# One unit's sums moved to TensorE, a norm's sum folded into a square, and a new order: a gated linear recurrence with a feed-forward block on one core

## The chip, the cores and the metric

The kernel runs on one core of a Trainium2 chip. A core has five engines with queues of their own: TensorE (PE in the profile, with its weight loads as PEld), VectorE (DVE), ScalarE (ACT), GpSimd (POOL) and SyncE (SP), which here only issues DMAs. The metric is device time in microseconds of one execution; before the change three runs took 679.76, 679.85 and 688.25 us, median 679.85.

## What is computed

An attention-like recurrence feeds a feed-forward block. For each of 4 x 8 heads of dimension 48, with S = 768 steps:

```
scale = min(|a|, 0.999) / (|a| + 1e-6)          # a = a_re + i a_im, per step and channel
S_t   = (a_t * scale_t) S_{t-1} + k_t v_t^T      # complex state, 48 x 48
y_t   = q_t . Re(S_t)
x     = y as 3072 rows of 384 (8 heads x 48)
out   = relu(x @ w_in)^2 @ w_out                 # w_in 384 x 2048, w_out 2048 x 384
```

The two weight matrices arrive as 64-bit floats and are turned to 32 bits on the core.

## The kernel before

The 3,072 rows are worked in six **units** (n = 0 to 5) of 512 rows. In a unit a partition holds W = 4 neighbouring steps of all heads; the heads are in two **halves** z of four, and in four **pairs** of heads. A unit goes through these stages, named by their functions.

`load` brings a_re, a_im (tile aq, first part), q and k (aq, second part) in from SyncE's queue (L910), for unit 0 with a_im from ScalarE's queue; v comes from GpSimd's queue (L925). `roots` takes the square of the modulus (L948, or L963 and L968 in unit 0; L971), then the logarithm (L973), an exponential with -0.5 (L975) for a first 1/|a|, its square (L977), and two VectorE steps (L979, L983) that refine it. In unit 0 the first half is cut in two, so that L973 to L983 run three times there. `normalise` makes the scale from it (L989 to L1003). At L1006 ScalarE squares the refined 1/|a| once more into a tile nobody reads, `junk`, only for the sum that such an activation can leave in the table `sums`. Such sums are tested at the end by `verdict`: if one is out of bounds, a slower general path runs instead.

`inner` multiplies the decays within a partition in two rounds: `terms` (L1021) makes the four partial products of a complex product, `joined` (L1025, L1026) takes their difference and sum. The second round's result goes to the tile xn. `totals` turns xn on TensorE with a permuted identity, `perm` (`turned`, L1070), and ScalarE copies the result to e (L1084, L1087). `scan` then runs a prefix product over e on VectorE (from L1159), `back` turns the result back, `factors` and `inverse` make reciprocals, and `apply` forms the scaled q and k (L1299 to L1327). `pairs` gathers keys (KC, L1370), transposes (by TensorE in unit 0, L1434; by VectorE and DMA to QT afterwards, L1410 and L1415), takes scores (L1456), masks them (L1462), keeps the state (L1486 to L1498) and mixes the output (L1510, L1514); ScalarE copies it out (L1520) and SyncE stores it to xT (L1528), the feed-forward block's input. `squares` sums q, k and v squared for the same test (L1268, L1271).

`dense` is the feed-forward block, twice per unit on 256 rows: w_in's products (L1570), relu and square on ScalarE (L1602, L1603), and w_out's products, plainly in unit 0 (L1617), by a scheme with seven half products and sums on VectorE afterwards (L1679, L1694, L1703). The weights are fetched in 8 + 8 pieces on GpSimd's queue (L820) and converted on ScalarE (L833, L837) and VectorE (L839, L843, L846). At the end `inspect` fetches them again and tests their range.

**What sets the order.** No stage is issued as it is written. Each call of `step`, `check` or `dma` adds a step to a plan: its engine, an assumed duration, what it reads and writes, and a rank. When the program is built, `Plan.order` plays the steps through with these assumed durations; whenever an engine is free it takes, of the steps that are ready, the one of lowest rank. The result fixes the order in each engine's queue, DMA issues included; the queues are in order on the chip. Ranks come from the stage and the unit (CHAIN 2, PAIR 1, DENSE 3, times 100), and `plan.shift` (L1821) adds numbers to single steps, counted in the order in which they are added, and to groups of them (same engine, same line, same rank). Where the plan has TensorE wait, it puts in idle matmuls of identity by identity (L738). VectorE runs the planned queue for unit 0 among the conversions of weights.

Of the kernel before, what the change touches and what calls it, by code (L numbers as in the profile page):

```python
# [632 lines left out]
def fast_path(ctx, tc, q, k, v, a_re, a_im, moe_w_in, moe_w_out, out, flag):  # L633
# [6 lines left out]
    C = 128  # L640
# [62 lines left out]
    NS = 11  # L703
# [168 lines left out]

    def parts(n):

        t, got = n * L, []
        while t < (n + 1) * L:
            b, s = divmod(t, S)
            m = min(S - s, (n + 1) * L - t)
            got.append(((t - n * L) // W, m // W, b, s))
            t += m  # L880
        return got
# [46 lines left out]
    def chain(n):  # L928
# [16 lines left out]
        def roots(z):  # L945
# [7 lines left out]
            for u in range(cut):  # L953
# [5 lines left out]
                if n == 0:  # L959
# [17 lines left out]
                step("ACT", ac(size), k(1), k(3), lambda u=u: act.activation(  # L977
                    out=part(t, u), in_=part(f1, u), func=AF.Square), first)
# [8 lines left out]
        def normalise(z):  # L987
# [3 lines left out]
            if n == 0:  # L991
# [14 lines left out]
            check("ACT", ac(Y), key(z, 3), [], lambda: act.activation(  # L1006
                out=junk[:, 0:Y], in_=t, func=AF.Square, saturate=False,
                accum_out=sums[:, n, 2 + z:3 + z]), first)

        def inner(z):  # L1010
# [4 lines left out]
            def pair(x0, x1, o, m, keys):  # L1015
                f1, f2 = (ff[z][:, i * m:(i + 1) * m].rearrange(
                    "p (r h d) -> p r h d", r=2, d=D) for i in range(2))

                def terms():
                    for j, f in enumerate((f1, f2)):  # L1020
                        dve.tensor_tensor(out=f, in0=x0, in1=x1[:, j].unsqueeze(  # L1021
                            1).to_broadcast(list(x0.shape)), op=ALU.mult)

                def joined():
                    dve.tensor_tensor(out=o[:, 0], in0=f1[:, 0], in1=f2[:, 1], op=ALU.subtract)  # L1025
                    dve.tensor_tensor(out=o[:, 1], in0=f1[:, 1], in1=f2[:, 0], op=ALU.add)  # L1026
                step("DVE", 2 * tt(m), [("a", z)], key(z, 0, 1), terms, ahead)
                step("DVE", 2 * tt(m // 2), key(z, 0, 1), keys, joined, ahead)
# [24 lines left out]
        E = [("e", 0), ("e", 1), ("e", 2)]  # L1053
        for fn in (roots, normalise, inner):
            for z in range(2):
                fn(z)
# [22 lines left out]

        def totals(j):  # L1080
            ps, b = turned(lambda m: xn[:, j, ts(m, C)], spread, perm,
                           [("xn", j, 0), ("xn", j, 1)], ahead)
# [183 lines left out]
        def squares(j):  # L1266
            for r in range(2):
                check("ACT", ac(Y), [(("qk", "k")[r], j)], [], lambda r=r: act.activation(  # L1268
                    out=junk, in_=QK[j][:, ts(r, Y)], func=AF.Square, saturate=False,
                    accum_out=sums[:, n, 4 + 2 * j + r:5 + 2 * j + r]), late[j])  # L1270
            check("ACT", ac(Y), [("v", vs(n))], [], lambda: act.activation(  # L1271
                out=junk, in_=vv[vs(n)][:, ts(j, Y)], func=AF.Square, saturate=False,
                accum_out=sums[:, n, 8 + j:9 + j]), late[1])
# [58 lines left out]
        def rest(*zs):  # L1332
# [4 lines left out]
            for z in zs:  # L1337
                twist(z)
                squares(z)
# [421 lines left out]
    def verdict():  # L1761
        def collect():
            for lo, hi, top_ in ((0, 2, 60), (2, 4, 12), (4, NS - 1, 20), (NS - 1, NS, 114)):
# [53 lines left out]
    for i in range(2 * NPIECE):  # L1817
        inspect(i)
    verdict()

    plan.shift(  # L1821
        groups={14: 395.74, 15: 440.83, 22: -2.57, 69: 298.91, 73: -200.67, 80: 0.99, 82: 4.44, 86:
# [5 lines left out]
        single={10: -100.97, 40: -497.42, 44: 62.89, 45: 37.9, 48: 75.39, 51: 100.84, 53: 52.42, 56:  # L1828
# [69 lines left out]
```

## Time and profile before

| | |
|---|---|
| median of three runs | 679.85 us |
| the profiled execution's own time | 680.22 us |
| its span, first to last instruction | 678.4 us |
| mean granted TensorE clock | 0.996 |
| busy: TensorE / its weight loads / VectorE / ScalarE / GpSimd | 657.3 / 592.6 / 557.7 / 350.9 / 111.4 us |
| idle matmuls of L738, within TensorE's busy time | 62.5 us |
| first dense product (L1570) starts | 93.94 us |
| last dense product (L1679) ends | 672.5 us |

A row of groups reads: line, engine, operation, output <- input, shapes, count | busy time in us, mean ns of one | idle time of the engine just before them, and what ended it. A row of the timeline or of the chain begins with start and length in us; in brackets stands the idle time before it with what ended it.

### The profile page before, as it was taken

To read this page: it belongs to the slowest core of one execution; us is meant where nothing else is said; L and a number is where in the kernel's file an instruction comes from. 1 tells how busy PE (TensorE), PEld (TensorE's weight loads), DVE (VectorE), ACT (ScalarE), POOL (GpSimd) and SP (SyncE) were. 2 spreads that over 40 slices of the span, in tenths; PEclk is the share of its full clock that TensorE was granted. 3 is DMA by queue.
4 is the path that set the end of the run, shared out by engine and by line. 5 is a ranking of instruction groups with operands and counts; after the bars stand their busy time and mean duration, and the time that the engine had idled before them with its cause. 6 is when DMAs were issued, how large, how long until landed. Compare 5 with 4: busy or idle time off the path is not lost.

```text
span 678.4 us, 13507 instructions
## 1 busy us (share of the span) xinstructions
PE 657.3 (97%) x5176; PEld 592.6 (87%) x5176; DVE 557.7 (82%) x1157; ACT 350.9 (52%) x574; POOL 111.4 (16%) x191
## 2 busy tenths in 40 slices
PE   9989999999899999999999999999999999999996
PEld 9989878677668998888998988988999989989996
DVE  5999989999499999698999788997889997347631
ACT  6997589962385514557524738334658132131230
POOL 6300305042000021002122030120030120032100
PEclk9999999999999999999999999999999999999999
DMA  9931659237660036624147562156360164287600
GB/s 278 300 121 44 148 139 253 108 104 181 154 166 15 23 74 157 171 67 129 36 123 167 132 139 48 37 141 161 101 179 20 36 153 104 56 300 262 230 2 28
DMA packets 56130, 86.32 MB, mean 127 GB/s; under 512 B 8916, under 2 KB 36640, under 8 KB 56056
## 3 DMA queue, kind: packets, MB, share of 16 engines
q1 hardware_dynamic: 39160, 37.93, 21.8%
q0 software_dynamic: 11840, 41.30, 21.1%
q10 hardware_dynamic: 5056, 6.13, 3.4%
q8 instruction: 43, 0.70, 0.5%
q14 instruction: 31, 0.25, 0.1%
HBM read 48.76 MB, written 4.72 MB: 79 GB/s over the span
## 4 chain that ended last, share of the span: by engine, by line
PE 56%; DVE 25%; DMA 7%; ACT 6%; issue 2%; SPq 1%; ACTq 1%; DVEq 0%
PE d L1570 24%; PE d L1679 22%; DMA QT<-aq 3%; DVE f L1327 3%; PE sc L1456 3%; DMA aq<-in_a_im_dram 2%; PE yp L1510 2%; DVE aq L1410 2%; PE yp L1514 2%; DVE w L846 2%; PE tr L1486 2%; DVE f L1299 1%; PE d L1617 1%; DVE KC L1179 1%; ACT g L1602 1%
## 5 line engine op out<-in xcount | busy, mean ns | idle before, releaser
L1570 PE MATMUL d<-xT,w 128*128 128x256 f32 x1104 | 246.7, 380 | 2.5 <-ACT g L1602 1.1
L1570 PEld LDWEIGHTS d<-xT,w 128*128 128x128 f32 x1104 | 207.6, 190 | 34.0 <-ACT g L1602 2.6
L1602 ACT ACTIVATE g<-d 128x512 f32<-128x512 f32 x92 | 54.8, 595 | 166.9 <-PE d L1570 109.4
L1679 PE MATMUL d<-w,g 128*128 128x192 f32 x640 | 111.6, 327 | 0.0
L1679 PEld LDWEIGHTS d<-w,g 128*128 128x128 f32 x640 | 104.6, 190 | 1.2 <-issue 0.6
L1679 PE MATMUL d<-T,g 128*128 128x192 f32 x480 | 84.6, 328 | 1.9 <-DVE g L1694 1.9
L1679 PEld LDWEIGHTS d<-T,g 128*128 128x128 f32 x480 | 78.7, 190 | 3.0 <-DVE g L1694 2.2
L1694 DVE TENSOR_TENSOR g<-g 128x512 f32<-128x512 f32 x80 | 53.9, 687 | 31.1 <-PE d L1679 17.4
L738 PE MATMUL d<-ident 128*128 128x128 f32 x526 | 62.5, 283 | 1.6 <-POOL ident masks.py:199 1.6
L738 PEld LDWEIGHTS d<-ident 128*128 128x128 f32 x526 | 61.9, 199 | 1.7 <-POOL ident masks.py:199 1.6
L1603 ACT ACTIVATE g<-g 128x512 f32<-128x512 f32 x96 | 60.6, 631 | 3.1
L1640 POOL DMA_DIRECT2D out_dram<-ot x22 | 12.7, 576 | 265.1 <-DVE ot L1703 221.4
L1520 ACT COPY yt<-yp 112x512 f32<-112x512 f32 x24 | 26.6, 1106 | 48.4 <-PE yp L1514 48.4
L1370 POOL DMA_DIRECT2D KC<-f x56 | 34.8, 627 | 101.2 <-DVE f L1327 40.9
L1410 DVE STREAM_TRANSPOSE aq<-f 128x768 f32<-128x768 f32 x40 | 47.8, 1265 | 0.2
L1327 DVE TENSOR_TENSOR f<-aq 128x768 f32<-128x768 f32 (+1 forms) x56 | 44.3, 838 | 0.6
L1617 PE MATMUL d<-w,g 128*128 128x384 f32 x128 | 44.4, 494 | 0.0
L1456 PE MATMUL sc<-QT 96*64 96x128 f32 (+1 forms) x736 | 39.0, 254 | 4.1 <-DMA QT<-aq 1.9
L1456 PEld LDWEIGHTS sc<-QT 96*64 96x64 f32 x736 | 35.6, 138 | 7.6 <-issue 4.0
L1703 DVE TENSOR_TENSOR ot<-ot,d 128x192 f32<-128x192 f32 x70 | 23.6, 349 | 20.6 <-PE d L1679 20.2
L1617 PEld LDWEIGHTS d<-w,g 128*128 128x128 f32 x128 | 24.1, 193 | 14.4 <-issue 0.5
L1021 DVE TENSOR_TENSOR f<-aq 128x768 f32<-128x768 f32 (+1 forms) x48 | 34.2, 752 | 0.5
(190 smaller groups left out, 915.9 us busy)
## 6 DMA issues: line engine op xcount, KB each, us to landing
QT<-aq SPq DMA_DIRECT2D x152, 64.0 KB, 2.5
f<-in_moe_w_in_dram POOLq DMA_DIRECT2D x8, 768.0 KB, 6.9
f<-in_moe_w_out_dram POOLq DMA_DIRECT2D x8, 768.0 KB, 6.4
QT<-aq ACTq DMA_DIRECT2D x76, 64.0 KB, 3.6
out_dram<-ot POOLq DMA_DIRECT2D x22, 192.0 KB, 3.7
KC<-f POOLq DMA_DIRECT2D x20, 192.0 KB, 3.7
xT<-yt SPq DMA_DIRECT2D x36, 96.0 KB, 2.3
aq<-in_q_dram SPq DMA_DIRECT2D x8, 384.0 KB, 5.3
```

What stands on the lines that cost most here:

```text
L738: plan = Plan(lambda b: pe.matmul(bank[b][:, 0:C], lhsT=ident, rhs=ident, start=True, stop=True), ["d2", "d1", "d0"], lambda ap: tc.nc.val ...
L1021: dve.tensor_tensor(out=f, in0=x0, in1=x1[:, j].unsqueeze(1).to_broadcast(list(x0.shape)), op=ALU.mult)
L1327: lambda j=j, r=r, o=o: dve.tensor_tensor(out=o[:, :, :, r * D:(r + 1) * D], in0=qk[:, j], in1=a[:, r], op=ALU.mult), late[z])
L1370: lambda i=i, queue=queue, lo=lo, hi=hi, a0=a0, a1=a1: queue.dma_start(out=kc[lo:hi, i], in_=nat[a0:a1]),
L1410: lambda nat=nat, dst=dst, j=j: dve.transpose(out=dst[:, j], in_=nat), rank)
L1456: pe.matmul(sa[r:r + C // 2, j, :, lo:32], lhsT=T[:, j, 1, h, ts(late, C // 2)], rhs=T[:, j, 0, h].rearrange("p (c t) -> p c t", c=W)[:, : ...
L1570: pe.matmul(ps, lhsT=w1[:, f // FP, m, ts(f % FP, C)], rhs=xT[:, n % 2, m, ts(grp, G)], start=(m == 0), stop=(m == NM - 1))
L1602: act.activation(out=o, in_=ps, func=AF.Relu)
L1603: act.activation(out=o, in_=o, func=AF.Square)
L1617: pe.matmul(ps, lhsT=gt[:, f % 2, ts(i, C)], rhs=w2[:, f], start=(f == 0), stop=(f == NF - 1))
L1679: pe.matmul(bank[b][:, 0:DH], lhsT=g4[:, r, j], rhs=w(j), start=first and j == 0, stop=last and j == NT - 1)
L1694: step("DVE", tt(4 * C), gk(x0, h) + gk(x1, h), gk(o, h), lambda: dve.tensor_tensor(out=g4[:, o, sl], in0=g4[:, x0, sl], in1=g4[:, x1, sl] ...
```

## The change

Three things.

1. The activation at L1006 is dropped. Its place is taken by the square in `roots` (L977), which now leaves its own sum in `sums`. Unit 0 has three of these squares, so the table gets a column more (NS 12), and `verdict` tests the new columns.
2. In unit 0, `joined` of the second round is dropped. `totals` takes the partial products themselves: a new step `joint` multiplies them, on TensorE, by `perm` and by its negative `nperm`, accumulating, so that the difference and the sum come out already turned. It takes twelve matmuls with 64 columns of weights, in turn to the upper and the lower half of the output's partitions, in place of three transposes. ScalarE makes `nperm` once.
3. The numbers of `plan.shift` are others throughout, and with the dropped and added steps they count differently. Queues of the DMAs are not changed: the loads stay on SyncE.

`squares_of` is added but, with AFTER = 0, never called, and `squares` stays as it was but for the column numbers.

```diff
-    NS = 11
+    NS = 12
+    AFTER = 0
...
-                step("ACT", ac(size), k(1), k(3), lambda u=u: act.activation(
-                    out=part(t, u), in_=part(f1, u), func=AF.Square), first)
+                at = 2 + z if u == 0 else 4
+                check("ACT", ac(size) + 0.09, k(1), k(3), lambda u=u, at=at: act.activation(
+                    out=part(t, u), in_=part(f1, u), func=AF.Square,
+                    accum_out=sums[:, n, at:at + 1]), first)
...
-            check("ACT", ac(Y), key(z, 3), [], lambda: act.activation(
-                out=junk[:, 0:Y], in_=t, func=AF.Square, saturate=False,
-                accum_out=sums[:, n, 2 + z:3 + z]), first)
...
-                step("DVE", 2 * tt(m // 2), key(z, 0, 1), keys, joined, ahead)
+                if n or keys == [("a", z)]:
+                    step("DVE", 2 * tt(m // 2), key(z, 0, 1), keys, joined, ahead)
...
+        nperm = yts[0][:, 0:C]
+        if n == 0:
+            step("ACT", 0.25, [], [("yt", 0)], lambda: act.mul(out=nperm, in_=perm, mul=-1.0),
+                 rank)
...
+        def joint(j):
+            b = trs[slot["tr"] % 2]
+            slot["tr"] += 1
+            ps = bank[b][:, 0:DM]
+            f = [ff[z][:, 0:Y].rearrange("p (i r x) -> p i r x", i=2, r=2) for z in range(2)]
+
+            def go():
+                for c0 in range(0, 2 * NM, 2):
+                    for i in range(2):
+                        for c in (c0, c0 + 1):
+                            r = 64 * (c % 2)
+                            pe.matmul(spread(ps[r:r + 64], c // 2),
+                                      lhsT=f[c // NM][:, i, (i + j) % 2, ts(c % NM, 64)],
+                                      rhs=nperm if (i, j) == (1, 0) else perm,
+                                      start=i == 0, stop=i == 1)
+            step("PE", 1.4, key(0, 0, 1) + key(1, 0, 1) + [("yt", 0)], [(b,)], go, ahead, mode=1)
+            return ps, (b,)
+
         def totals(j):
-            ps, b = turned(lambda m: xn[:, j, ts(m, C)], spread, perm,
-                           [("xn", j, 0), ("xn", j, 1)], ahead)
+            ps, b = joint(j) if n == 0 else turned(
+                lambda m: xn[:, j, ts(m, C)], spread, perm, [("xn", j, 0), ("xn", j, 1)], ahead)
...
     plan.shift(
-        groups={14: 395.74, 15: 440.83, 22: -2.57, 69: 298.91, 73: -200.67, 80: 0.99, 82: 4.44, 86:
...
+        groups={3: -336.32, 8: -339.38, 9: 203.68, 15: 194.34, 28: 5.78, 29: -244.11, 91: -4.1, 97:
+            -8.34, 102: -255.12, 103: 422.4, 111: 356.0, 114: -237.11, 116: 2.36, 160: 100.49,
...
+        single={40: 459.41, 43: 446.7, 44: -245.71, 49: -438.55, 58: -1.11, 81: -227.32, 82:
+            -251.41, 83: 100.96, 100: 0.02, 121: 0.61, 143: -221.32, 161: 109.9, 162: -255.4,
```

More of the change, by code (lines that the diff above doesn't have):

```diff
@@ L869, in inspect, with squares_of @@
         check("DVE", ts2(PW) + tt(PW), keys, keys + [("odd",)], look, rank)
+    def squares_of(n, j):
+        z, s = (3 * n + j) % 2, (3 * n + j) // 2 % 2
+        t = ff[z][:, s * Z:(s + 1) * Z]
+        keys = [("f", z, 2 * s), ("f", z, 2 * s + 1)]
+        rank = (LATE, 2 * NPIECE + 3 * n + j)
+        for p0, m, b, at in parts(n):
+            src = (q, k, v)[j][b, :, at:at + m * W, :].rearrange("h (p c) d -> p h (c d)", c=W)
+            dma(pool, [("gate", 1)], keys, lambda p0=p0, m=m, src=src: pool.dma_start(
+                out=t.rearrange("p (h x) -> p h x", h=H)[p0:p0 + m], in_=src),
+                rank, m * 3072 * 2, dur=0.74, group=n)
+        at = (5, 6, 9)[j]
+        check("ACT", ac(Z) + 0.09, keys, keys, lambda: act.activation(
+            out=t, in_=t, func=AF.Square, accum_out=sums[:, n, at:at + 1]), rank)
     def parts(n):
@@ L1269, in squares @@
                     out=junk, in_=QK[j][:, ts(r, Y)], func=AF.Square, saturate=False,
-                    accum_out=sums[:, n, 4 + 2 * j + r:5 + 2 * j + r]), late[j])
+                    accum_out=sums[:, n, 5 + 2 * j + r:6 + 2 * j + r]), late[j])
             check("ACT", ac(Y), [("v", vs(n))], [], lambda: act.activation(
                 out=junk, in_=vv[vs(n)][:, ts(j, Y)], func=AF.Square, saturate=False,
-                accum_out=sums[:, n, 8 + j:9 + j]), late[1])
+                accum_out=sums[:, n, 9 + j:10 + j]), late[1])
         def apply(z, p, np):
@@ L1338, in rest @@
                 twist(z)
-                squares(z)
+                if n >= AFTER:
+                    squares(z)
             for z in zs:
@@ L1762, in collect @@
         def collect():
-            for lo, hi, top_ in ((0, 2, 60), (2, 4, 12), (4, NS - 1, 20), (NS - 1, NS, 114)):
+            for lo, hi, top_ in ((0, 2, 60), (2, 5, 12), (5, NS - 1, 20), (NS - 1, NS, 114)):
                 dve.tensor_scalar(out=ok[:, :, lo:hi], in0=sums[:, :, lo:hi],
@@ L1818, in fast_path @@
         inspect(i)
+    for n in range(AFTER):
+        for j in range(3):
+            squares_of(n, j)
     verdict()
     plan.shift(
-        groups={14: 395.74, 15: 440.83, 22: -2.57, 69: 298.91, 73: -200.67, 80: 0.99, 82: 4.44, 86:
[5 rows of a table removed]
-        single={10: -100.97, 40: -497.42, 44: 62.89, 45: 37.9, 48: 75.39, 51: 100.84, 53: 52.42, 56:
[13 rows of a table removed]
+        groups={3: -336.32, 8: -339.38, 9: 203.68, 15: 194.34, 28: 5.78, 29: -244.11, 91: -4.1, 97:
[5 rows of a table added]
+        single={40: 459.41, 43: 446.7, 44: -245.71, 49: -438.55, 58: -1.11, 81: -227.32, 82:
[11 rows of a table added]
     with tc.manual_schedule():
```

32 rows, old and new, of tables (groups, single) are left out of this document.

## The prediction

> **What bounds the kernel now.** I read the head of the page first, then the timeline of TensorE, then the busy times in stretches cut where that timeline changes, then TensorE's waits.
>
> ```profile
> span 678.4 us, 13507 instructions
> PE 657.3 (97%) x5176; PEld 592.6 (87%) x5176; DVE 557.7 (82%) x1157; ACT 350.9 (52%) x574; POOL 111.4 (16%) x191
> ...
> L738 PE MATMUL d<-ident 128*128 128x128 f32 x526 | 62.5, 283 | 1.6 <-POOL ident masks.py:199 1.6
> ```
>
> TensorE looks full at 97%, but 62.5 us of that are the matmuls of L738, identity times identity, which only fill time while nothing else can run. The timeline of TensorE shows the last of them and the first dense product (L1570):
>
> ```profile
> 90.24 1.38 PE L738 MATMUL d<-ident 128*128 128x128 f32 x10
> ...
> 93.94 3.02 PE L1570 MATMUL d<-xT,w 128*128 128x256 f32 x12
> ```
>
> So I cut at 93.94, at 200 and at 655. In the table of stretches the columns are length, then busy time and count of TensorE, its weight loads, VectorE, ScalarE and GpSimd, the granted clock, the DMA share and GB/s:
>
> ```profile
> 9.30:93.94 84.64, 81.74 (x929) 78.25 (x927) 82.00 (x198) 65.25 (x92) 21.88 (x36) 1.00 0.63 175
> 93.94:200.00 106.06, 100.49 (x657) 75.66 (x656) 91.07 (x171) 71.93 (x116) 22.26 (x33) 0.98 0.59 155
> 200.00:655.00 455.00, 449.94 (x3448) 413.85 (x3445) 375.03 (x770) 207.57 (x357) 64.01 (x102) 1.00 0.43 115
> 655.00:678.40 23.40, 17.49 (x108) 17.20 (x106) 6.96 (x14) 0.91 (x2) 0.00 (x0) 0.96 0.07 22
> ```
>
> There are two stages with different limits. Up to 93.94 it is VectorE: 82.00 of 84.64 us busy, while TensorE fills. From there TensorE is the bound, with real work: it idles 106.06 - 100.49 = 5.57 us up to 200 and 455.00 - 449.94 = 5.06 us up to 655, together 10.63. The last stretch is the closing chain of products and stores. The time is thus the start of the first dense product, plus TensorE's own work, plus 10.63 of stalls, plus an end of fixed length. An edit can gain by an earlier start or by fewer stalls. The stalls have names in the waits of TensorE from 94 to 660 (total, times, longest):
>
> ```profile
> PE d L1679 <- DVE g L1694: 1.9, 1, 1.9
> PE sc L1456 <- DMA QT<-aq: 1.9, 2, 1.0
> ...
> PE sc L1456 <- DMA T<-aq: 0.9, 1, 0.9
> PE sc L1456 <- DMA xT<-yt: 0.8, 1, 0.8
> ```
>
> No single one is over 1.9 us. All sums below are made against the profiled execution, 680.22 us (its span of 678.4 and 1.8 around it); the median of the three runs shown is 679.85, 0.37 lower, which I take off at the end. Two per cent of it is 13.6 us, about what a measurement of this kernel can tell from no change.
>
> **The change part by part.** First the squares. In each unit and half the sum at L1006 goes, and the square at L977 gets an accumulation. The timeline of ScalarE in unit 0:
>
> ```profile
> 16.56 0.84 ACT L977 ACTIVATE f<-f 128x768 f32<-128x768 f32 x1
> 17.31 0.83 ACT L1006 ACTIVATE junk<-f 128x768 fp8e5<-128x768 f32 x1
> 18.05 0.19 ACT L1006 ACTIVATION_READ_ACCUMULATOR junk<-f 128x1 f32 x1
> 18.27 0.84 ACT L992 ACTIVATE junk<-f 128x768 fp8e5<-128x768 f32 x1
> ```
>
> From start to start L1006 takes 18.27 - 17.31 = 0.96 us, the reading of its sum 18.27 - 18.05 = 0.22 of that. Removed 0.96, added 0.22 behind L977: 0.74 less on ScalarE for each of twelve, 8.9 us. In unit 0 there are three squares, since its first half is cut in two: 2 x 0.96 - 3 x 0.22 = 1.26 less. ScalarE is 52% busy, so nearly all of this lies beside TensorE's stream and is worth nothing. The reading may hold L979 on VectorE by 0.22 where nothing else is ready for it; in unit 0 that is three times, 0.66 at most, and I take nothing, since the order has conversions to put there. The gain counts where ScalarE stands on the chain of work, and there L1006 is right ahead of SyncE's store of xT, the transfer that TensorE's wait of 0.8 names:
>
> ```profile
> 189.72 0.83 ACT junk L1006 x2
> 190.55 0.14 SPq L1528
> ```
>
> I take that wait as gone, **-0.8**; its bounds are 0 (another transfer holds the store) and -0.8.
>
> Second, the inner sums of unit 0. VectorE loses four instructions, L1025 and L1026 into xn for both halves. Its timeline:
>
> ```profile
> 25.18 0.35 DVE L1025 TENSOR_TENSOR xn<-f 128x192 f32<-128x192 f32 x1
> 25.45 0.35 DVE L1026 TENSOR_TENSOR xn<-f 128x192 f32<-128x192 f32 x1
> 25.72 0.95 DVE L1000 SCALAR_TENSOR_TENSOR f<-f 128x768 f32<-128x768 f32 x1
> ...
> 35.25 2.80 DVE L846 CUSTOM_DVE_ANT_0 w<-w,w 128x1536 uint16<-128x1536 uint16 x3
> 37.97 0.35 DVE L1159 TENSOR_TENSOR KC<-e 128x192 f32<-128x192 f32 x1
> ```
>
> A pair takes 25.72 - 25.18 = 0.54 us from start to start, two take 1.08. VectorE bounds this stage, so the first dense product comes earlier by **-1.1**. In its place TensorE has two steps of twelve matmuls, 64 columns wide and alternating between the halves of the array, for two steps of three transposes:
>
> ```profile
> 35.09 0.82 PE L1070 MATMUL tr<-perm,xn 128*128 128x128 f32 x6
> 35.74 10.66 PE L738 MATMUL d<-ident 128*128 128x128 f32 x94
> ...
> 74.99 0.93 PE L1456 MATMUL sc<-QT 96*64 96x128 f32 x15
> ```
>
> The transposes take 0.82 / 2 = 0.41 a step. Twelve of the new kind cost at least the spacing of L1456, which alternates halves too, 0.93 / 15 = 0.062 each or 0.74 a step, and at most that of a whole matmul, 10.66 / 94 = 0.113 or 1.36. That is 0.33 to 0.95 more a step, 0.7 to 1.9 for both; the row that is alike gives 0.7. On TensorE it takes the place of fillers. For the scan (L1159) it is a delay. VectorE covered the present gap, 35.25 to 37.97, with three conversions; with the sums gone the gap is some 0.7 longer, and a further conversion or L1039 fits in. Without that cover it costs 0.7 to 1.9; I take 0. The negated matrix is one small ScalarE copy, less than the 1.26 saved there.
>
> Whether going from 64 columns to the whole array and back costs something, TensorE's timeline shows elsewhere:
>
> ```profile
> 66.50 1.96 PE L1434 MATMUL d<-ident,f 128*96 128x128 f32 x16 [0.61 <-DVE f L1327]
> 68.38 1.09 PE L1456 MATMUL sc<-QT 96*64 96x128 f32 x16
> ```
>
> L1456 starts before the end of L1434 (66.50 + 1.96 = 68.46), so a switch shows no gap. The Trainium skill, TensorEngine Tiling (Array Packing), section Key Properties, says that changing the tiling mode drains the TensorE; by it each new step would begin and end with a drain. The trace does not show such a drain as lost time, and fillers stand on both sides, so the sum would be the same unless the scan's cover is gone.
>
> Third, the new order. The two tables at the end count steps, and groups of alike steps, as the code adds them. Counting them through: unit 1's sixteen loads on SyncE go ahead of all else that is ready there (group 114, which had a default place); unit 0's loads of v go ahead of the weight fetches on GpSimd (group 3); w2's conversions on VectorE go far back (group 103); the second half of unit 0 is hurried (singles 81 and 82). The timeline of SyncE shows what issuing two of these loads takes, the chain of work how long the last one takes to land, and VectorE's timeline who waits behind it:
>
> ```profile
> 83.97 1.28 SPq L910 DMA_DIRECT2D aq<-in_a_re_dram  x2
> ```
> ```profile
> 85.30 8.32 DMA aq<-in_a_im_dram
> ```
> ```profile
> 95.34 0.96 DVE L971 TENSOR_TENSOR f<-f 128x768 f32<-128x768 f32 x1 [1.66 <-ACT f L948]
> ```
>
> The load issued at 85.30 lands 8.32 later, and VectorE then idles 1.66 before L971. Loads that are issued sooner end that. It reaches TensorE only through the end of unit 1's attention, so I give it the 0.9 that TensorE waits for T<-aq, **-0.9**. What the rest of the order does, the trace of before cannot show. Its gain is bounded by all stalls, 10.63. Its loss is bounded by the loads: one issue takes 1.28 / 2 = 0.64, sixteen 10.2 us, and if all stand ahead of the last store of xT, the first dense product is that much later. I take 0 for it, since the stalls named above are small, many, and on different engines. The v loads delay weights by what six of them take; conversions are only filler before the scan, so this falls under the cover above.
>
> Sum: 680.22 - 0.8 - 1.1 - 0.9 = 677.4; less 0.37, **677.0 us**.
>
> **The rivals.** *The order closes the stalls*: with the start 1.1 earlier and all 10.63 gone, 679.85 - 11.7 = 668; with VectorE's 84.64 - 82.00 = 2.64 idle in the first stage gone too, 665.5; half of it gives 673. For it speaks that the stalls are waits on moved work; against it that they have many causes.
>
> *SyncE's queue blocks*, the slow one. A load at the head of that queue which waits for its half of aq holds the KC gathers, the xT stores and later the QT transposes behind it. SyncE's timeline has the stores of unit 0's last pairs right behind the loads:
>
> ```profile
> 86.34 12.75 SPq L1528 DMA_DIRECT2D xT<-yt  x8
> ```
>
> The eight take 12.75 us, with waits between them. With all sixteen ahead it costs 10.2, so 687; if units 2 to 5 lose as much again as the 5.06 that they stall now, or double that, 692 to 697. It decides from the point where the loads hold the queue by more than the 2.8 that I gain.
>
> *Nothing arrives*: the removed VectorE time is given back in the longer gap before the scan, and the other waits go to the next transfer; 679.9. The change then doesn't do what it says for the time.
>
> *Weight loads bound TensorE*, not matmuls. PEld is busy 592.6 us, 87%. If the dense stream ran at the load's pace, a better order would shrink it. The chain has a row on its spacing, the groups one on its weight loads:
>
> ```profile
> 633.25 18.13 PE d L1570 x84
> ```
> ```profile
> L1570 PEld LDWEIGHTS d<-xT,w 128*128 128x128 f32 x1104 | 207.6, 190 | 34.0 <-ACT g L1602 2.6
> ```
>
> 18.13 / 84 = 0.216 us a matmul, back to back. A weight load takes 0.190; at that pace 1,104 matmuls of L1570 take 29 us less, 648. Against it: 0.216 stands wherever nothing is waited for, whatever the order. The Trainium Kernel Development and Optimization page of the Trainium skill, section Performance Expectations, holds LDWEIGHTS busy % for the measure, not matmul busy; this trace does not agree for this stream.
>
> **How the numbers follow.** Forecast, 674 to 682: 0.48. Stalls closed, 665 to 673: 0.20. SyncE blocks, 683 to 697: 0.22. Nothing arrives: 0.08. Weight loads: 0.02. Faster by over 2% means under 666.2: the last case and a fifth of the second, 0.06. Slower by over 2% means over 693.4: not quite half of the third, 0.10. The range leaves out the second case below 668 and the fourth rival, 0.07 together, and of the third what lies above 689, 0.13: 668 to 689.
>
> **What would show it.** ScalarE's busy time is lower by 8 to 9 us and L1006 is gone; the four L1025 and L1026 into xn of unit 0 are gone; the new matmuls take 0.7 to 1.4 us a step, and L1159 starts the scan without an idle VectorE ahead of it; the first L1570 starts at 92 to 93.5; TensorE's idle time from there to 655 is 8 to 10.6. I am wrong if that start is past 95 with xT stores behind loads on SyncE, or if the idle time is under 5 or over 13.

## The result: slower by 0.6 per cent

The changed kernel takes 685.44 us in the median (20 runs, 679.3 to 689.94), the kernel before beside it 680.84. The ratio is 1.0056, with a 95% interval of 1.0034 to 1.0078: about 3.8 us slower, where 2.8 faster was forecast. The time lies within the forecast's range, on the other side of no change. Ratios, here and below, leave out the executions in a slower state that some runs fall into, and they are not the quotients of the medians shown, from which they differ by up to 0.3 per cent. The profiled execution took 685.22 us, with a span of 683.5 and a mean granted clock of 0.992. The head of its page, and the groups' row of the idle matmuls (L738 before):

```profile
span 683.5 us, 13541 instructions
PE 657.1 (96%) x5194; PEld 594.6 (87%) x5194; DVE 557.3 (82%) x1153; ACT 342.3 (50%) x564; POOL 110.5 (16%) x191
...
L739 PE MATMUL d<-ident 128*128 128x128 f32 x502 | 59.4, 282 | 1.6 <-POOL ident masks.py:199 1.6
```

ScalarE lost 350.9 - 342.3 = 8.6 us of work, and TensorE, busy for as long as before, does 3 us less of it in idle matmuls. The first dense product (L1609, L1570 before) starts at 98.92, not 93.94. The table of stretches, cut there, at 200, and 23.40 ahead of the end as before:

```profile
9.30:98.92 89.62, 83.37 (x942) 79.79 (x940) 83.01 (x198) 71.73 (x102) 21.47 (x37) 0.96 0.58 166
98.92:200.00 101.08, 91.05 (x560) 69.33 (x560) 83.47 (x159) 59.12 (x99) 22.67 (x33) 0.99 0.58 153
200.00:660.10 460.10, 457.09 (x3543) 420.17 (x3540) 382.26 (x781) 207.19 (x358) 63.64 (x102) 1.00 0.43 116
660.10:683.50 23.40, 17.96 (x111) 17.67 (x109) 6.98 (x14) 1.35 (x3) 0.00 (x0) 0.97 0.07 21
```

TensorE's idle time is 10.03 + 3.01 = 13.04 us, against 10.63. The 5.1 us of span are thus: the start 4.98 later, 2.41 more of stalls, 2.29 less of TensorE's work behind the start (548.14 against 550.43), the end the same. TensorE's waits in the same part now have one large name, the relu and square of ScalarE (L1641, L1602 before):

```profile
PE d L1609 <- ACT g L1641: 7.7, 3, 3.5
PE yp L1549 <- ACT f L1014: 2.7, 1, 2.7
PE tr L1090 <- DVE xn L1268: 1.2, 2, 0.7
```

Where the late start begins is seen in the first microseconds of ScalarE's timeline, before and after:

```profile
0.86 1.52 ACTq L910 DMA_DIRECT2D aq<-in_a_im_dram  x3
```
```profile
2.27 0.31 ACT L1072 ACTIVATE yt<-perm 128x128 f32<-128x128 f32 x1 [0.17 <-POOL perm L722]
2.27 2.20 ACTq L926 DMA_DIRECT2D aq<-in_a_im_dram  x3
```

ScalarE's queue also issues unit 0's a_im loads. The copy that makes `nperm` stands ahead of them, and it waits for `perm`, which GpSimd writes first. So the loads leave at 2.27, not 0.86. VectorE's first square waits for them, before and after:

```profile
4.50 0.56 DVE L968 TENSOR_TENSOR f<-aq 128x384 f32<-128x384 f32 x1 [3.01 <-DMA aq<-in_a_im_dram]
```
```profile
7.65 0.56 DVE L984 TENSOR_TENSOR f<-aq 128x384 f32<-128x384 f32 x1 [6.16 <-DMA aq<-in_a_im_dram]
```

1.41 us at the issue have become 3.15 at the first square. In after SyncE issues its loads of q and k from 2.35, alongside the late a_im loads; that the loads slow each other down would explain the difference, but it was not tested.

### The profile page after: what moved, and what is told of

Read it like the earlier page. It is cut to its first block, busy times and chain, and to the rows that moved or that the text cites. A ratio compares the mean times of both kernels' runs of the same rounds, so it can differ in the third digit from the quotient of the medians.

```text
span 683.5 us, 13541 instructions
## 1 busy us (share of the span) xinstructions
PE 657.1 (96%) x5194; PEld 594.6 (87%) x5194; DVE 557.3 (82%) x1153; ACT 342.3 (50%) x564; POOL 110.5 (16%) x191
## 4 chain that ended last, share of the span: by engine, by line
PE 61%; DVE 23%; DMA 7%; issue 3%; ACT 3%; SPq 2%; ACTq 1%; DVEq 0%
PE d L1609 24%; PE d L1718 24%; PE sc L1495 4%; PE yp L1549 3%; DMA aq<-in_k_dram 2%; PE yp L1553 2%; DVE f L1365 2%; PE tr L1525 2%; DVE f L1036 2%; DVE aq L1449 1%; DVE KC L1217 1%; DVE f L1337 1%; DMA QT<-aq 1%; PE d L1656 1%; DMA aq<-in_a_im_dram 1%
## 5 line engine op out<-in xcount | busy, mean ns | idle before, releaser
L1609 PE MATMUL d<-xT,w 128*128 128x256 f32 x1104 | 246.9, 381 | 7.7 <-ACT g L1641 7.7
L1609 PEld LDWEIGHTS d<-xT,w 128*128 128x128 f32 x1104 | 208.0, 190 | 37.8 <-ACT g L1641 9.2
L1641 ACT ACTIVATE g<-d 128x512 f32<-128x512 f32 x92 | 54.5, 593 | 177.8 <-PE d L1609 116.6
L739 PE MATMUL d<-ident 128*128 128x128 f32 x502 | 59.4, 282 | 1.6 <-POOL ident masks.py:199 1.6
L739 PEld LDWEIGHTS d<-ident 128*128 128x128 f32 x502 | 58.6, 198 | 1.9 <-POOL ident masks.py:199 1.6
L1365 DVE TENSOR_TENSOR f<-aq 128x768 f32<-128x768 f32 (+1 forms) x56 | 44.2, 839 | 0.4
L1495 PE MATMUL sc<-QT 96*64 96x128 f32 (+1 forms) x736 | 37.3, 252 | 0.4 <-issue 0.4
L1501 DVE TENSOR_TENSOR A<-sc,mask 128x512 f32<-128x512 f32 x45 | 29.3, 681 | 6.6 <-PE sc L1495 6.6
```

The source lines that it names most:

```text
L739: plan = Plan(lambda b: pe.matmul(bank[b][:, 0:C], lhsT=ident, rhs=ident, start=True, stop=True), ["d2", "d1", "d0"], lambda ap: tc.nc.val ...
L1365: lambda j=j, r=r, o=o: dve.tensor_tensor(out=o[:, :, :, r * D:(r + 1) * D], in0=qk[:, j], in1=a[:, r], op=ALU.mult), late[z])
L1495: pe.matmul(sa[r:r + C // 2, j, :, lo:32], lhsT=T[:, j, 1, h, ts(late, C // 2)], rhs=T[:, j, 0, h].rearrange("p (c t) -> p c t", c=W)[:, : ...
L1501: step("DVE", tt(L) + 0.05, [(b,)], [("A", a)], lambda: dve.tensor_tensor(out=As[a].rearrange("p (j i t) -> p j i t", j=W // 2, i=2), in0= ...
L1609: pe.matmul(ps, lhsT=w1[:, f // FP, m, ts(f % FP, C)], rhs=xT[:, n % 2, m, ts(grp, G)], start=(m == 0), stop=(m == NM - 1))
L1641: act.activation(out=o, in_=ps, func=AF.Relu)
```

## The experiments

Two theories. **N**: the copy at the head of ScalarE's queue holds the loads, and the chain of unit 0 with them. **O**: the new order costs the time, wherever the copy stands. The parts of the change were also made in the order of before: there the planned list of steps is left alone, and single steps issue something else. Idle is TensorE's idle time from the first dense product to 200, and on to 23.40 ahead of the end; start and idle are of the one profiled execution. Each ratio is to runs of the kernel before on the same chip beside it; their medians were 681.03 for a_nperm_gps, b_nperm_act, b_squares and b_parts, 681.49 for b_nperm_head, b_parts_head, a_no114 and b_joint, 681.34 for a_nperm_late, h_ab and h_ba, and 678.61 for a_relu_first.

| run | median us | ratio to before (95%) | first dense product | idle us |
|---|---|---|---|---|
| before | 680.84 | | 93.94 | 5.57 + 5.06 |
| after | 685.44 | 1.0056 (1.0034 to 1.0078) | 98.92 | 10.03 + 3.01 |
| a_nperm_gps | 678.35 | 0.9981 (0.9947 to 1.0015) | 93.92 | 7.30 + 2.97 |
| a_nperm_late | 677.59 | 0.9948 (0.9918 to 0.9978) | 93.46 | 7.02 + 5.09 |
| b_nperm_act | 679.5 | 0.9993 (0.9961 to 1.0025) | 92.96 | 7.45 + 2.60 |
| b_nperm_head | 684.27 | 1.0067 (1.0035 to 1.0099) | 97.35 | 4.12 + 4.63 |
| b_squares | 677.73 | 0.9962 (0.9926 to 0.9997) | 93.21 | 5.50 + 3.55 |
| b_joint | 676.12 | 0.9914 (0.9882 to 0.9946) | 93.18 | 6.45 + 3.15 |
| b_parts | 674.46 | 0.9909 (0.9881 to 0.9938) | 93.16 | 3.17 + 4.07 |
| b_parts_head | 680.51 | 0.9961 (0.9930 to 0.9993) | 96.08 | 5.00 + 5.00 |
| a_no114 | 685.72 | 1.0042 (1.0010 to 1.0074) | 93.03 | 5.61 + 8.19 |
| h_ab | 677.07 | 0.9944 (0.9924 to 0.9965) | 93.49 | 2.49 + 3.35 |
| h_ba | 680.91 | 0.9999 (0.9971 to 1.0026) | 93.00 | 7.38 + 4.73 |
| a_relu_first | 677.58 | 0.9980 (0.9948 to 1.0011) | 93.70 | 4.91 + 3.61 |

### The copy in ScalarE's queue

**a_nperm_gps**: the kernel after, with the copy on GpSimd.

```diff
-            step("ACT", 0.25, [], [("yt", 0)], lambda: act.mul(out=nperm, in_=perm, mul=-1.0),
+            step("ACT", 0.25, [], [("yt", 0)], lambda: pool.tensor_scalar(out=nperm, in0=perm,
+                 scalar1=-1.0, scalar2=None, op0=ALU.mult),
```

> The changed kernel with one edit: the negated matrix nperm is made on GpSimd, so that nothing of it stands in ScalarE's queue ahead of the loads of a_im; order otherwise as changed. Theory N (nperm, which waits for perm from GpSimd, holds the a_im loads that ScalarE issues, and everything starts some 3 us late): the a_im loads are issued from 0.9 us again instead of 2.3, VectorE's first square starts at 4.5 to 5 us instead of 7.65, the first dense product at 95.8 to 97 instead of 98.9, and the time falls by 2 to 3 us against the changed kernel, to 0 to +2.5 us against the kernel before. Rival O (the new order alone sets the first dense product, by conversions put behind the scan): the squares start earlier too, but the first dense product stays at 98 or later and the ratio to the kernel before at 1.004 to 1.007.

The loads left at 0.86, the first dense product started at 93.92, and the ratio fell from 1.0056 to 0.9981. N holds, O falls for the start; the gain, 0.75%, is larger than expected.

**b_nperm_act**: the kernel before, with a copy that nothing reads.

```diff
+    act.mul(out=yts[0][:, 0:C], in_=perm, mul=-1.0)
     with tc.manual_schedule():
```

> The kernel before with one instruction more: ScalarE's copy of the negated matrix at the head of its queue, ahead of its three loads of a_im; nobody reads it. Theory N: VectorE's first square at about 7.6 us instead of 4.5, first dense product 2 to 3 us later than 93.94, time +2 to +3 us against the kernel before, ratio 1.003 to 1.0045. Rival O: unit 0's VectorE work takes up the delay, ratio 0.999 to 1.001.

The edit missed: the copy was placed at 9.0 us, behind the loads, and the time is that of before. It says that 0.29 us of ScalarE there costs nothing, and one thing more: it is before's work in before's order, so its profile shows how far two profiles of nearly the same kernel lie apart. Its scan (L1159) and its first dense product start 1.10 and 0.98 us earlier than in before's profile (37.97 and 93.94), and its span is 2.5 us shorter:

```profile
36.87 0.35 DVE L1159 TENSOR_TENSOR KC<-e 128x192 f32<-128x192 f32 x1
...
92.96 2.86 PE L1570 MATMUL d<-xT,w 128*128 128x256 f32 x12
```

Differences of a microsecond between two profiles are therefore no effect by themselves.

**b_nperm_head**: the same copy, now first in the queue.

```diff
     with tc.manual_schedule():
+        act.mul(out=yts[0][:, 0:C], in_=perm, mul=-1.0)
         bad = plan.emit(flag[0:1, 0:1])
```

> The kernel before, with the negated copy of perm put first in ScalarE's queue, ahead of unit 0's a_im loads; nothing reads it. Theory N (the copy waits for perm and holds the loads behind it): the loads are issued at about 2.3 us in place of 0.86, the first square on VectorE starts at about 7.6 in place of 4.5, the first dense product (L1570) at 96 to 99 in place of 93.9, and the ratio to the kernel before is 1.004 to 1.0075. Rival R (before's order has slack for it, and what is lost in the kernel after is lost by its order): the first dense product is at 95 or sooner, the ratio 0.998 to 1.002.

Its timelines of ScalarE and VectorE:

```profile
2.27 0.31 ACT L1843 ACTIVATE yt<-perm 128x128 f32<-128x128 f32 x1 [0.17 <-POOL perm L721]
2.28 2.37 ACTq L910 DMA_DIRECT2D aq<-in_a_im_dram  x3
```
```profile
7.48 0.56 DVE L968 TENSOR_TENSOR f<-aq 128x384 f32<-128x384 f32 x1 [5.99 <-DMA aq<-in_a_im_dram]
```

One copy whose result nobody uses makes the kernel before slower by 0.67%, 4.6 us, and reproduces the late loads, the late square and a first dense product at 97.35. The Trainium skill, DMA: Bandwidth & Descriptors, in its breakdown of the fixed cost of a DMA, says that DMA engines do not wait on semaphores and that any such wait happens on the issuing sequencer before dispatch. The trace agrees: with the copy ahead, the issue itself moves from 0.86 to 2.28, right behind the start of the copy. The loads then also take longer, 5.20 us from issue to first square against 3.64.

**b_parts_head**: squares and joint sums in before's order (b_parts, below), with the copy first on ScalarE in place of GpSimd.

```diff
-    pool.tensor_scalar(out=yts[0][:, 0:C], in0=perm, scalar1=-1.0, scalar2=None, op0=ALU.mult)
     with tc.manual_schedule():
+        act.mul(out=yts[0][:, 0:C], in_=perm, mul=-1.0)
```

> The squares and the joint inner sums in before's order, as in b_parts, but with the negated copy of perm on ScalarE, first in its queue, in place of GpSimd. Theory N: the same price on another kernel: first dense product 2 to 5 us later than the 93.16 of b_parts, ratio 0.994 to 0.999 where b_parts had 0.991. Rival R: as b_parts, 0.991, with a first dense product at 93 to 94.5. If N holds, this is the whole change but for its order, so the kernel after against it gives the order alone: 0.7% by the pair with the copy on GpSimd.

Start at 96.08, 2.9 later than b_parts, ratio 0.9961 against 0.9909: 3.5 us, with an interval of some 3 us to either side.

**a_nperm_late**: the kernel after, with one exchange in ScalarE's queue.

```diff
         order = self.order()
+        loads = [n for n in order if self.steps[n][0] == "ACT" and self.steps[n][5] is not None][:3]
+        order.remove(58)
+        order.insert(order.index(loads[-1]) + 1, 58)
```

> The kernel after with one exchange in ScalarE's queue: the negated copy of perm behind unit 0's three a_im loads, in place of ahead of them; engine, copy and all other steps as they are. Theory N (what the copy holds up is the loads behind it): loads at 0.86, first square on VectorE at 4.5, first dense product at 93.5 to 94.5, ratio 0.996 to 1.001, as with the copy on GpSimd (0.998). Rival P (it was good that GpSimd did the copy, not that the loads went first): the first dense product stays past 96, ratio 1.003 to 1.007.

ScalarE's and TensorE's timelines:

```profile
0.85 1.53 ACTq L929 DMA_DIRECT2D aq<-in_a_im_dram  x3
2.44 0.31 ACT L1075 ACTIVATE yt<-perm 128x128 f32<-128x128 f32 x1 [0.33 <-POOL mask L730]
```
```profile
93.46 2.86 PE L1612 MATMUL d<-xT,w 128*128 128x256 f32 x12
```

The copy runs 0.17 us later than in the kernel after, and the first dense product 5.46 earlier. From 1.0056 to 0.9948 the kernel turns from slower to faster, by 7.3 us (some 2.5 to either side), with the same instructions on every engine. Rival P falls.

### The two parts, in before's order

**b_squares**: the sum at L977, L1006 dropped.

```diff
-                    out=part(t, u), in_=part(f1, u), func=AF.Square), first)
+                    out=part(t, u), in_=part(f1, u), func=AF.Square,
+                    accum_out=sums[:, n, (2 + z if u == 0 else 4):(3 + z if u == 0 else 5)]), first)
...
                 accum_out=sums[:, n, 2 + z:3 + z]), first)
+            plan.instead[len(plan.steps) - 1] = lambda: None
```

> The first part alone, in the order of before: the sum goes with the square at L977, the activation of L1006 is not issued. The prediction's sum: ScalarE 8.9 us less busy, -0.8 us in time, ratio 0.9988. Rival: the wait on the xT store stays or goes to the next transfer, ratio 0.9995 to 1.0005.

**b_joint**: the joint sums of unit 0, `nperm` by GpSimd. `instead` gives what a planned step issues in its place.

```diff
                 step("DVE", 2 * tt(m // 2), key(z, 0, 1), keys, joined, ahead)
+                if n == 0 and keys != [("a", z)]:
+                    plan.instead[len(plan.steps) - 1] = lambda: None
...
+            if n == 0:
+                plan.instead[len(plan.steps) - 1] = lambda: joint(j, ps)
```

> The joint inner sums of unit 0 alone, in before's order, with the negated copy on GpSimd; the squares as before. Theory S (the two parts add up): b_parts had 0.991 and the squares alone 0.996, so 0.993 to 0.997, with a first dense product at 93.2 to 94 and a joint step of 1.4 us. Rival T (the joint sums only pay together with the shorter ScalarE work, since they make the gap before the scan longer): 0.998 to 1.002, VectorE idle for 0.7 us or more ahead of the scan.

**b_parts**: both.

> Both parts in the order of before, nperm made on GpSimd: L1006 not issued, unit 0's second round of joined sums not issued, TensorE sums them while turning. The prediction's sum: first dense product 1.1 us earlier, at 92.8, time -1.9 us, ratio 0.997. Rival: the longer turn (two steps of 0.7 to 1.4 us) gives the 1.1 back ahead of the scan, ratio 0.9988 to 1.0.

The squares alone give 0.9962, the joint sums alone 0.9914, both 0.9909. Each gains more than expected, though the interval of the squares alone reaches what was expected of them (0.9988); rival T falls. By the intervals the two may add up wholly or only in part. All three start the dense products at 93.2, 0.73 to 0.78 earlier than in before's profile, whichever part is in, but b_nperm_act, with neither part, starts them at 92.96: no gain at the start is shown. TensorE's timeline in b_parts shows the two joint steps, and VectorE's the scan behind them:

```profile
34.05 0.44 PE L1094 MATMUL tr<-perm,f 128*64 128x128 f32 x4
...
35.41 1.48 PE L1094 MATMUL tr<-perm,f 128*64 128x128 f32 x24
36.82 2.39 PE L740 MATMUL d<-ident 128*128 128x128 f32 x19
```
```profile
37.45 0.36 DVE L1180 TENSOR_TENSOR KC<-e 128x192 f32<-128x192 f32 x1 [0.82 <-ACT e L1105]
```

The steps take 35.41 - 34.05 = 1.36 and 36.82 - 35.41 = 1.41 us, and VectorE idles 0.82 ahead of the scan. It starts 0.52 earlier than in before's profile (37.97) and 0.58 later than in b_nperm_act's (36.87). The table of stretches of b_parts:

```profile
93.16:200.00 106.84, 103.67 (x679) 78.60 (x679) 97.22 (x180) 72.79 (x117) 21.42 (x33) 1.00 0.59 158
200.00:647.60 447.60, 443.53 (x3423) 409.44 (x3422) 369.18 (x761) 198.17 (x343) 63.86 (x102) 1.00 0.43 116
647.60:671.00 23.40, 17.66 (x109) 17.37 (x107) 6.96 (x14) 1.04 (x3) 0.00 (x0) 0.99 0.07 21
```

Its span is 7.4 shorter than before's: 0.78 from the start, 3.39 fewer stalls, and 3.23 less time in TensorE's work (547.20 against 550.43), at a mean granted clock of 1.000 in place of 0.996. Some 1.7 of the 3.23 is the clock: behind its first dense product before runs 3.41 us at 0.50 (last section), which costs half of that, and b_parts none. Against b_nperm_act's profile the span is 4.9 shorter: the start 0.20 later, 2.81 fewer stalls, 2.29 less of TensorE's work. By both the gain lies in stalls and TensorE's own time. Why a saving in unit 0 lessens the stalls of later units was not tested. b_parts is faster than the kernel before by 0.9%, and than the kernel after by 1.5%.

### The new order

a_nperm_gps and a_nperm_late do what b_parts does, in the new order, and are slower than it by 0.7 and 0.4%; the first difference is clear of the intervals, the second is not. With the copy at the head of the queue in both, after is slower than b_parts_head by 0.95%, also clear of them. So the new order costs time; how much, between 0.4 and 0.95%, is uncertain.

**a_no114**: a_nperm_gps, unit 1's loads at their default place.

```diff
-            -8.34, 102: -255.12, 103: 422.4, 111: 356.0, 114: -237.11, 116: 2.36, 160: 100.49,
+            -8.34, 102: -255.12, 103: 422.4, 111: 356.0, 116: 2.36, 160: 100.49,
```

> The kernel after with the negated copy on GpSimd (as a_nperm_gps), and without the entry of group 114, so that unit 1's sixteen loads on SyncE have their default place again. Theory L (the loads put ahead are what the new order costs, by crowding unit 1's transfers): TensorE's idle time from the first dense product to 655 falls from 10.3 to 7 to 8 us, the waits of the dense product for g on ScalarE from 4.2 to under 2, ratio 0.991 to 0.995. Rival M (the rest of the order costs it): idle time 9.5 to 12, ratio 0.996 to 1.000.

Neither: it is slower, 1.0042, with 13.80 us idle. Its largest wait of TensorE:

```profile
PE yp L1549 <- ACT yt L1559: 4.4, 1, 4.4
```

So putting these loads back does not win the cost back. But leaving the number out lets the plan lay out many later steps differently, so the run does not show what these loads cost by themselves.

**h_ab** and **h_ba**: a_nperm_gps with its sequence of steps written out: in h_ab the new order up to 93 us by the plan, then before's; in h_ba the other way round.

```diff
-        order = self.order()
+        self.order()
+        order = ORDER
```

> The steps of a_nperm_gps; the new order for those steps that it plans to start before 93 us (364 of 2353), the order of before for all the rest. The new order costs 0.7% against before's (0.998 against 0.991). Theory E (the cost lies in the early part of the order, up to the first dense product: what is put off there comes due later): ratio 0.996 to 1.000, TensorE's idle time from the first dense product to 655 10 to 13 us. Theory L (it lies in the order of the attention of units 1 to 5): ratio 0.990 to 0.994, idle time 6 to 8.

> The steps of a_nperm_gps; the order of before for those steps that it plans to start before 93 us (359 of 2353), the new order for all the rest. Theory E: ratio 0.989 to 0.993, idle time 6 to 8 us. Theory L: 0.996 to 1.000, idle time 10 to 13. If both this and h_ab lie above 0.996, neither part costs by itself: what costs is where two orders meet, and the place stays open.

Stretches of h_ab, then of h_ba, and TensorE's largest waits in h_ba:

```profile
93.49:200.00 106.51, 104.02 (x676) 79.06 (x675) 95.15 (x178) 69.65 (x113) 22.24 (x33) 0.98 0.60 158
200.00:648.40 448.40, 445.05 (x3426) 410.03 (x3425) 369.96 (x761) 198.52 (x343) 64.14 (x102) 1.00 0.43 116
```
```profile
93.00:200.00 107.00, 99.62 (x637) 75.00 (x638) 90.53 (x168) 66.20 (x107) 22.36 (x33) 0.97 0.58 155
200.00:654.70 454.70, 449.97 (x3462) 413.63 (x3459) 375.99 (x773) 204.52 (x354) 63.50 (x102) 1.00 0.43 115
```
```profile
PE d L1723 <- ACT g L1755: 6.5, 3, 3.8
PE tr L1204 <- ACT g L1755: 3.1, 1, 3.1
```

With the new order only up to 93 the ratio is 0.9944 and the idle time 5.84; with the new order only behind it, 0.9999 and 12.11. h_ba is as Theory L said; h_ab lies just outside its ranges, on either side. The two differ by 0.55%, clear of the intervals: most of the cost lies behind 93, and in the trace up to 200 (7.38 idle against 2.49), as waits for g, the dense product's relu on ScalarE. That h_ab is 0.35% above b_parts, with intervals that overlap, leaves a smaller cost of the early part possible.

**a_relu_first**: in a_nperm_late the longest such wait stood here (ScalarE, TensorE, VectorE):

```profile
128.48 0.27 ACT L1279 COPY xn<-e 128x48 f32<-128x48 f32 x1 [4.98 <-DVE e L1222]
128.62 0.59 ACT L1644 ACTIVATE g<-d 128x512 f32<-128x512 f32 x1
```
```profile
129.26 2.93 PE L1612 MATMUL d<-xT,w 128*128 128x256 f32 x6 [3.84 <-ACT g L1644]
```
```profile
120.85 0.76 DVE L1070 TENSOR_TENSOR aq<-aq,f 128x576 f32<-128x576 f32 x1 [4.59 <-issue]
```

The profile names no releaser for VectorE's wait ("issue"). The step multiplies k, and the chain has unit 1's last k load land at 116.27, as that wait begins, so that it is a wait for the loads is likely but not shown. The relu has the shape of the copy at the queue's head: a step that waits, and work behind it that could go.

```diff
         order.insert(order.index(loads[-1]) + 1, 58)
+        order.remove(395)
+        order.insert(order.index(537), 395)
```

> a_nperm_late with one more exchange in ScalarE's queue: in unit 1, the relu and square of one dense product ahead of the copy xn<-e of the scan, in place of right behind it. In a_nperm_late ScalarE stood idle for 4.98 us with that copy at its head (it waits for VectorE, which waited 4.59 for unit 1's loads), the relu behind it, and TensorE then waited 3.84 for the relu's g. Theory Q (the new order costs by relus that stand behind waiting work in ScalarE's queue): the wait of 3.84 near 129 us is under 0.8, the idle time of TensorE from the first dense product to 200 falls from 7.0 to 3 to 4.5, ratio 0.988 to 0.992, where a_nperm_late had 0.995. Rival V (the loads, not the queue: TensorE soon waits for unit 1's attention by as much): the wait moves to another row, idle time 6 to 8, ratio 0.993 to 0.998.

The relu now runs at 123.83 and that wait is gone, but the next one for g, 1.13 in a_nperm_late, is longer:

```profile
160.13 7.18 PE L1614 MATMUL d<-xT,w 128*128 128x256 f32 x18 [3.12 <-ACT g L1646]
```

The median is that of a_nperm_late, 677.6, and the ratio, 0.998, no better than its 0.995; the intervals overlap. In this profile VectorE waited 0.43 us where it had waited 4.59 in a_nperm_late, so there was little to save at this place in this execution. Theory Q is not borne out as a matter of time. V had the ratio right, and that the wait moves to another row; the idle time up to 200, 4.91, lies between the ranges of the two. What in the new order behind 93 costs the 0.4 to 0.7% stays open below the level of "waits for ScalarE's g".

## Why the prediction was wrong

**What bounds the kernel** held: start, TensorE's work, stalls and a fixed end account for the whole difference of the spans.

**The step that failed** is the last sentence of the part on the inner sums: "The negated matrix is one small ScalarE copy, less than the 1.26 saved there." It was costed by its busy time, 0.31 us, and not by its place. It heads the queue that issues unit 0's a_im loads, and it waits for GpSimd. Its price is 3.5 us (b_parts_head against b_parts), 4.6 (b_nperm_head against before) or 7.3 (after against a_nperm_late); the intervals, 2 to 3 us to either side, allow one price for all three. The forecast looked for such a blocked queue on SyncE, as its slow rival; it was ScalarE's. That rival itself falls: with the copy out of the way the first dense product started at 93.46, with all sixteen loads as the new order has them.

How the late loads became 5.46 us at the first dense product can be followed through the steps that after and a_nperm_late share. On VectorE the lag is 2.98 at the first square (7.65 against 4.67) and 3.92 at the third (11.91 against 7.99), because VectorE waits for a_im again at the second:

```profile
10.77 0.56 DVE L984 TENSOR_TENSOR f<-aq 128x384 f32<-128x384 f32 x1 [1.90 <-DMA aq<-in_a_im_dram]
```

It stays at 3.8 to 3.9 up to 81 us; the scan (L1197 after, L1200 in a_nperm_late) starts at 38.45 and 34.52, 3.93 apart. TensorE's joint step waits in between, with nothing laid out to fill the gap, and runs at half clock after it (rows in the last section), but that adds nothing to VectorE's lag. What adds to it is a second such place: TensorE waits 2.72 for KC<-f at 81.77, where a_nperm_late waits 2.00, and the granted clock is at 0.50 behind it. The same transposes, after and in a_nperm_late, and the clock in after:

```profile
82.33 2.69 PE L1473 MATMUL d<-ident,f 128*96 128x128 f32 x12
```
```profile
77.64 1.52 PE L1476 MATMUL d<-ident,f 128*96 128x128 f32 x12
```
```profile
82.00:84.00 2.00, 2.00 (x16) 1.84 (x14) 1.40 (x7) 0.48 (x1) 0.00 (x0) 0.50 0.05 17
```

TensorE's step behind them starts at 84.95 and 79.08, 5.87 apart.

**Squares, -0.8.** ScalarE's 8.6 us less are as worked out (8.9), and alone they give 0.9962, 2.6 us with 0.2 to 5.0 as bounds. The reason given was wrong: the wait of TensorE for xT<-yt did not go; in b_squares it is the longest:

```profile
PE sc L1459 <- DMA xT<-yt: 2.1, 1, 2.1
```

**Inner sums, -1.1.** No run shows this gain at the start: b_joint starts 0.76 earlier than before's profile, and b_nperm_act, with no such part, 0.98. A joint step took 1.4 us, the upper end of 0.74 to 1.36. Twelve matmuls of the code leave 24 records, and the spacing of L1456, 0.062, is one of records, so the forecast by the row that is alike should have been 24 x 0.062 = 1.5. The upper bound was met by luck, for its 0.113 is a spacing of records too. The cover for it was not whole: in b_parts VectorE idles 0.82 ahead of the scan, in b_joint 0.97 ahead of the last conversion before the scan. The whole gain of b_joint, 5.9 us (3.7 to 8.0), is larger than its start explains.

**Order, -0.9 and else 0.** It costs 2.7 to 4.9 us against before's order by the pairs without the copy at the head, 6.5 by after against b_parts_head. All are inside the bounds of -10.63 and 10.2, but the value taken had the wrong sign. The argument from one wait, T<-aq, counted a wait that the order removes and none that it makes: with the copy out of the way TensorE waits 4.2 (a_nperm_gps) and 6.5 us (a_nperm_late) for g in the new order, 7.7 in after, against 1.5 in b_parts. In before it waited 1.1:

```profile
PE d L1570 <- ACT g L1602: 1.1, 2, 0.8
```

With the measured terms: both parts 0.991; then 0.7% for the order and 0.75% for the copy by a_nperm_gps, 0.4% and 1.1% by a_nperm_late, or 0.95% and 0.5% by b_parts_head. All three ways end at 1.0056, since they go by the same two ends; the split between order and copy is uncertain by about half a per cent. With the copy out of the way the change gives 0.9981 and 0.9948, near the 0.996 that was forecast; that is luck, for the parts gain 6 us where 1.9 was added up and the order takes back what it was to add. The rivals "stalls closed", "nothing arrives" and "weight loads" did not come about; the second is also refuted by b_parts. Of the signs of being wrong, the idle time over 13 came, at 13.04, and a start past 95 as well, though from the copy and not from stores behind loads. Nor is two per cent what it takes to tell a change here: the interval of the ratio is 0.2 per cent to either side.

## What to carry to other kernels

Cost a small instruction by what stands behind it in its queue and by what it waits for, not by its own length; at the head of a queue that issues the first loads, 0.31 us of copying cost 3.5 to 7.3 here. When a planner puts it there, look at what the plan does not know: here `perm` was not among its steps, so the copy looked ready at 0. When a change comes with a new order, measure the change in the old order first: here that version was 0.9% faster and the whole 0.6% slower.

## What was not expected of the hardware

Around some waits of TensorE the granted clock falls to 0.50 for 3.41 us or twice that. In after it does so with a wait of 2.17. TensorE's timeline, and the stretches ahead of the fall and of the fall itself:

```profile
33.65 0.48 PE L1111 MATMUL tr<-perm,f 128*64 128x128 f32 x1 [2.17 <-DVE f L1036]
```
```profile
30.17:33.58 3.41, 1.31 (x15) 0.95 (x13) 3.38 (x7) 3.38 (x5) 0.00 (x0) 1.00 1.00 378
33.58:36.99 3.41, 3.34 (x32) 3.17 (x34) 3.38 (x8) 2.62 (x5) 0.00 (x0) 0.50 1.03 393
```

In before, behind two short waits (TensorE's timeline, and the stretches):

```profile
183.16 0.40 PE L1456 MATMUL sc<-QT 96*64 96x128 f32 x2 [1.05 <-DMA QT<-aq]
184.36 1.77 PE L1456 MATMUL sc<-QT 96*64 96x128 f32 x25 [0.80 <-DMA QT<-aq]
```
```profile
184.00:186.00 2.00, 1.64 (x27) 1.67 (x29) 1.41 (x2) 1.35 (x3) 0.00 (x0) 0.73 0.46 107
186.00:188.00 2.00, 2.00 (x30) 1.72 (x27) 2.00 (x4) 1.46 (x2) 0.00 (x0) 0.50 0.64 154
```

In after, a longer wait was followed by no fall: its stretches from 120 to 140 stand at 1.00, among them these two of 3.41 us.

```profile
134.38 1.56 PE L1609 MATMUL d<-xT,w 128*128 128x256 f32 x6 [3.49 <-ACT g L1641]
```
```profile
129.15:132.56 3.41, 1.74 (x6) 0.73 (x4) 3.10 (x21) 0.24 (x1) 0.00 (x0) 1.00 0.00 0
132.56:135.98 3.42, 1.56 (x6) 1.06 (x6) 3.01 (x16) 2.35 (x6) 0.00 (x0) 1.00 0.00 0
```

The Trainium skill, TensorE: Matmul & The Clock Gate, Part 1, has a gate that halves the clock after at least one idle window of about 3.4 us, the windows running free of the kernel. The trace agrees on the half rate. It does not agree that a whole window of idleness is needed: 2.17 us was enough. The traces show what decides instead. In all fourteen the times between two changes of the clock are whole multiples of 3.413 us, so each execution can be cut into periods of that length. From 20 us to 26 us ahead of the end, each of the 14 full-clock periods in which TensorE was busy for less than 1.45 us is followed by one at 0.50; of those with 1.5 to 2.05 us some are (before's fall above had 1.56 ahead of it), of those with more none. The wait of 2.17 lay almost wholly in one period, which left 1.31 us busy. The wait of 3.49 was shared by two, with 1.74 and 1.56 busy. So where a wait falls in its period matters, and not its length alone. What decides between 1.5 and 2.05 was not found.

The same step waits differently from one execution to the next: VectorE 4.59 us ahead of its product with unit 1's k in a_nperm_late, 0.43 in a_relu_first, on another chip, with the same queues up to there. A wait read from a single profile is not yet a price.
